# Keys and batch 1's x by the crossbar, six half groups at the start of block 1, and one more last store on ScalarE's queue, in a pooled attention and maxout kernel

## Chip, cores and metric

One core of one Trainium2 chip. The metric is the device time of one execution in microseconds, the median of several.

## The reference

```python
# q, k, v: (8 batches, 8 heads, 576, 64); pool = 8, so 72 pooled keys and values
k_p = k.reshape(B, H, Sp, pool, D).mean(axis=3)
v_p = v.reshape(B, H, Sp, pool, D).mean(axis=3)
attn = softmax(q @ k_p.T / sqrt(D))
x = (attn @ v_p) as (4608 tokens, 512)
h = maximum(maximum(x @ w1, x @ w2), x @ w3)      # 512 -> 768
out = h @ w_out                                   # 768 -> 512
```

## The kernel before

The kernel makes the output in nine blocks of 512 tokens. Block n computes the hidden layer of its tokens (18 groups of four 512-column matmuls) and the projection (four tiles), and in the slots between these groups it puts the attention of batch n+1: keys `k`, eight heads' scores `s`, five values `v` and their transposes `x`, and the query transpose `T` of batch n+2. The loads of batch n+2 are issued by GpSimd and released by the first matmul group of block n.

```python
    def turn_k(b):                       # transpose pooled keys on TensorE, copy to kz
        pkt = keys(b, TR)
        for par in range(2):
            fill_kz(b, par, 0, H, pkt,
                    nc.scalar.copy if b == 1 else nc.vector.tensor_copy)

    def turn_x(b, c0, keep, xn, tag, evac=nc.scalar.copy):
        if b > 1:                        # crossbar, issued by SyncE
            nc.sync.dma_start_transpose(out=xT[...], in_=xn...)
            return
        # otherwise four TensorE transposes into PSUM and one copy
    # in do():
            elif name[0] == "T":
                qTs[b] = sb2.tile([128, 2 * NG, 128], BF16, name="qT", tag="qT")
                nc.sync.dma_start_transpose(
                    out=qTs[b], in_=qbs[b].rearrange("p hp t d -> p (hp t d)"))
    # ... in hidden(): which hidden chunks run on half the tokens first
        if n == 0:
            parts = [(0, 1, 0, 128), (0, 1, 128, 256), (1, 2, 0, 256), (0, 2, 256, NB),
                     (2, JCH, 0, NB)]
        elif n == 1:
            parts = [(0, 1, 0, 256), (0, 1, 256, NB), (1, JCH, 0, NB)]
    # ... in project(): each 128-token tile is stored as two halves by SyncE
                    (nc.scalar if last and u else nc.sync).dma_start(
                        out=dst[:, GS[g], c], in_=osb[64 * u:64 * u + 64, c])
    # ...
    def plan(n):                         # slot: [(batch, steps)]
        b, i = n + 1, 3 * (n == 1)
        got = {0: [], 3: [], 3 + i: [(b, "k")]}
        got.update({5 + i + h: [(b, f"s{h}")] for h in range(H)})
        got[12 + i].append((b + 1, "T"))
        got.update({15 + i + c: [(b, f"v{c} x{c}")] for c in range(5)})
        ...
    def pool_work(n, mm):                # called in slot 0 of block n
        if n + 2 < B:
            after([load_k(n + 2)], mm)
            load_q(n + 2)
            load_v(n + 2)
        if n == 1:
            fold_v(2)
        if n + 2 < B:
            fold_k(n + 2, nc.gpsimd)
            fold_v(n + 2)
```

The softmax here doesn't subtract the row's maximum and nothing guards it: scores larger than these inputs give would overflow.

## Time and profile before

| What | Value |
|---|---|
| Time | 242.75 us median of 3 runs (242.71 to 242.88) |
| Profiled span | 241.0 us |
| TensorE busy | 230.9 us, 96% |
| Next engine (VectorE) | 131.7 us, 55% |
| Start to block 0 | 16.96 us |
| Blocks 0, 1, 2 | 31.73, 24.75, 24.28 us |
| Blocks 3 to 6 | 24.27 to 24.37 us each |
| Block 8 and the end | 25.35 us |

A block's length here and below is the distance between the first hidden-layer matmuls (`pw`) of two successive blocks in TensorE's timeline. A wait for x just before a block's first matmul thus counts for the block before it.

### The profile page before, as it was taken

What the parts mean: (1) busy time and instruction counts of PE and PEld (TensorE: products, weight loads), DVE (VectorE), ACT (ScalarE), POOL (GpSimd) and SP (SyncE); (2) the same over time, 40 slices, a digit from 0 to 9 for tenths busy, and PEclk for the clock granted to TensorE, in tenths of its full rate; (3) what the DMA queues carried; (4) which work ended last, traced back from release to release, by engine and by line L of the source; (5) the groups of instructions that cost most, each with busy time, mean ns of one, the idle gap of its engine ahead of it and who ended that gap; (6) DMA issues with size and microseconds to landing.
All of it is one profiled execution on the core that took longest, in us unless ns stands there. A gap on an engine that the chain in (4) does not pass through costs nothing.

```text
span 241.0 us, 4221 instructions
## 1 busy us (share of the span) xinstructions
PE 230.9 (96%) x1609; PEld 122.7 (51%) x1609; DVE 131.7 (55%) x239; ACT 100.1 (42%) x173; POOL 123.7 (51%) x91
## 2 busy tenths in 40 slices
PE   7698999999999999999999999999999999999992
PEld 3376555575554555455545554555455544444441
DVE  6856754665583558354836483648364834504530
ACT  2373247546513651365235523552355232142121
POOL 8864276989997479638880979286500000000000
PEclk9999999999999999999999999999999999999999
DMA  7999999999948995699769987997640253043006
GB/s 135 188 198 206 196 202 208 169 166 241 184 97 153 222 166 120 128 194 197 131 125 156 227 176 133 193 192 135 133 93 0 69 123 85 3 108 66 0 20 154
DMA packets 51939, 34.29 MB, mean 142 GB/s; under 512 B 32144, under 2 KB 46480, under 8 KB 51920
## 3 DMA queue, kind: packets, MB, share of 16 engines
q0 software_dynamic: 17088, 17.11, 45.5%
q1 hardware_dynamic: 34672, 16.79, 34.3%
q8 instruction: 12, 0.20, 0.3%
q10 hardware_dynamic: 160, 0.13, 0.2%
q14 instruction: 7, 0.06, 0.1%
HBM read 34.60 MB, written 9.44 MB: 183 GB/s over the span
## 4 chain that ended last, share of the span: by engine, by line
PE 89%; DVE 5%; ACT 2%; DMA 2%; issue 1%; DVEq 0%
PE pw L295 55%; PE po L331 19%; PE psc L203 6%; PE pav L238 4%; DMA kt<-in_k_dram 2%; PE pxt L229 1%; DVE kf L362 1%; ACT et L208 1%; DVE t L304 1%; PE pkt L174 1%; PE pvp L156 1%; DVE xn L246 1%; PE pqt L167 1%; DVE kp L366 1%; DVE kf L364 1%
## 5 line engine op out<-in xcount | busy, mean ns | idle before, releaser
L295 PE MATMUL pw<-xT,mw 128*128 128x512 f16 (+2 forms) x696 | 155.6, 364 | 0.8 <-ACT xT L233 0.7
L295 PEld LDWEIGHTS <-mw 128*128 128x128 f16 x696 | 61.8, 98 | 56.2 <-issue 1.0
L304 DVE TENSOR_TENSOR t<-t,pw 128x512 f16<-128x512 f16 (+2 forms) x58 | 37.8, 651 | 71.0 <-PE pw L295 43.7
L301 ACT CAST t<-pw 128x512 f16<-128x512 f32 (+2 forms) x58 | 32.3, 556 | 56.1 <-PE pw L295 54.8
L331 PE MATMUL po<-mwo,hT 128*128 128x512 f16 (+1 forms) x222 | 50.7, 373 | 0.0
L208 ACT ACTIVATE et<-psc 72x576 f16<-72x576 f32 (+2 forms) x62 | 40.7, 662 | 20.9 <-PE psc L203 20.7
L307 DVE TENSOR_TENSOR hT<-t,pw 128x512 f16<-128x512 f16 (+2 forms) x58 | 37.7, 650 | 9.0 <-PE pw L295 5.3
L336 ACT COPY osb<-po 128x512 f32<-128x512 f32 (+1 forms) x36 | 20.9, 580 | 47.7 <-PE po L331 43.7
L135 POOL TENSOR_TENSOR half<-vt 72x2048 f32<-72x2048 f16 x7 | 28.4, 4060 | 10.0 <-DMA vt<-in_v_dram 9.9
L331 PEld LDWEIGHTS <-hT 128*128 128x128 f16 x222 | 20.3, 97 | 21.3 <-DVE hT L307 2.4
L135 POOL TENSOR_TENSOR half<-kt 96x1536 f32<-96x1536 f16 x6 | 18.5, 3085 | 23.4 <-DMA kt<-in_k_dram 23.3
L246 DVE TENSOR_TENSOR xn<-pav,rcp 128x512 f16<-128x512 f32 x39 | 27.0, 691 | 1.5 <-DVE rcp L244 0.2
L136 POOL TENSOR_TENSOR half<-half 72x1024 f32<-72x1024 f32 (+1 forms) x13 | 27.2, 2096 | 1.0
L203 PE MATMUL psc<-qT,kz 128*128 128x64 bf16 (+3 forms) x192 | 25.9, 246 | 0.4 <-DVE kz L179 0.3
L203 PEld LDWEIGHTS <-kz 128*128 128x128 bf16 x192 | 17.8, 98 | 15.7 <-DVE kz L179 1.5
L238 PEld LDWEIGHTS <-et 72*128 72x128 f16 x312 | 15.2, 98 | 7.6
L238 PE MATMUL pav<-vp,et 72*128 72x65 f16 x312 | 16.5, 194 | 0.0
L244 DVE RECIPROCAL rcp<-pav 128x8 f32<-128x8 f32 x39 | 7.9, 204 | 9.4 <-PE pav L238 9.3
L139 POOL TENSOR_TENSOR kp<-half 96x384 bf16<-96x384 f32 x12 | 11.7, 993 | 0.5
L179 DVE COPY kz<-pkt 64x576 bf16<-64x576 bf16 (+1 forms) x14 | 9.9, 711 | 2.9 <-PE pkt L174 2.7
L79 POOL DMA_DIRECT2D vt<-in_v_dram x10 | 8.0, 804 | 2.9 <-DMA qb<-in_q_dram 2.2
L139 POOL TENSOR_TENSOR vp<-half 72x512 f16<-72x512 f32 x7 | 8.9, 1268 | 0.5
(48 smaller groups left out, 79.1 us busy)
## 6 DMA issues: line engine op xcount, KB each, us to landing
out_dram<-osb SPq DMA_DIRECT2D x70, 128.0 KB, 2.4
kt<-in_k_dram POOLq DMA_DIRECT2D x7, 576.0 KB, 7.4
qb<-in_q_dram POOLq DMA_DIRECT2D x7, 576.0 KB, 12.2
vt<-in_v_dram POOLq DMA_DIRECT2D x7, 576.0 KB, 15.0
mw<-in_moe_w_dram POOLq DMA_DIRECT2D x9, 256.0 KB, 9.3
mwo<-in_moe_w_out_dram POOLq DMA_DIRECT2D x1, 768.0 KB, 18.1
qb<-in_q_dram POOLq DMA_DIRECT2D x2, 288.0 KB, 7.0
xT<-xn SPq DMA_TRANSPOSE x30, 2.4
```

The source lines that it names most:

```text
L135: e.tensor_tensor(out=f, in0=t[:, :, 0:4, :], in1=t[:, :, 4:8, :], op=ALU.add)
L136: e.tensor_tensor(out=f[:, :, 0:2, :], in0=f[:, :, 0:2, :], in1=f[:, :, 2:4, :], op=ALU.add)
L203: nc.tensor.matmul(out, kz_all[b % 2][:, f % 2, h, :], qTs[b][:, n + i0:n + i1, 64 * (h % 2):64 * (h % 2) + 64], start=True, stop=True)
L208: nc.scalar.activation(out=out, in_=in_, func=FT.Exp, scale=1.0 / 64.0)
L238: nc.tensor.matmul(pav[:, h // 4, 65 * (h % 4):65 * (h % 4) + 65], ets[b][:, h, c0:c0 + 128], vp_all[:, b, h, :], start=True, stop=True)
L246: nc.vector.tensor_tensor(out=xn, in0=pv[:, :, :, 0:D], in1=rcp.to_broadcast([128, 2, 4, D]), op=ALU.mult)
L295: mm = nc.tensor.matmul(pw, w_sb[wi][:, kc, bass.ts(jc, 128)], xT[:, kc, col], start=(kc == 0), stop=(kc == KCH - 1))
L301: nc.scalar.copy(out=t, in_=pw)
L304: nc.vector.tensor_tensor(out=t1, in0=t, in1=pw, op=ALU.max)
L307: nc.vector.tensor_tensor(out=hT[:, jc, c0:c1], in0=t, in1=pw, op=ALU.max)
L331: nc.tensor.matmul(po, hT[:, jc, bass.ts(mm, 128)], wo_sb[:, jc, c], start=(jc == 0), stop=(jc == JCH - 1))
L336: nc.scalar.copy(out=osb[:, c], in_=po)
```

## The change

The intent is to take work off TensorE, which bounds the kernel: the key transposes of batches 3 to 7 and the x transposes of batch 1 move to the crossbar, that is, to DMA transfers that transpose (`dma_start_transpose`, issued by SyncE; step `Z` is the one of the keys). Batch 1's attention moves later in block 0. To give its x time to arrive, block 1 opens with six half groups (groups on 256 of the 512 tokens; three before) ahead of the other half of the tokens, and batch 2's attention sits eight slots late in block 1. Of the last tile's four stores ScalarE's queue issues three instead of two, and both of the tile's copies go to VectorE. Of block 0 the cut below shows the end alone.

```diff
     def turn_k(b):
-        pkt = keys(b, TR)
+        pkt = keys(b, TR) if b < 3 else kTs[b]
...
-                    nc.scalar.copy if b == 1 else nc.vector.tensor_copy)
+                    nc.vector.tensor_copy if b == 2 else nc.scalar.copy)
     def turn_x(...):
-        if b > 1:
+        if b > 0:
     # in do():
+            elif name[0] == "Z":
+                kTs[b] = sb2.tile([128, 6, 96], BF16, name="kT", tag="kT")
+                nc.sync.dma_start_transpose(
+                    out=kTs[b], in_=kps[b].rearrange("p i a d -> p (i a d)"))
     # in hidden():
-            parts = [(0, 1, 0, 128), (0, 1, 128, 256), (1, 2, 0, 256), (0, 2, 256, NB),
-                     (2, JCH, 0, NB)]
+            parts = [(0, 1, 0, 128), (0, 1, 128, 256), (1, 3, 0, 256), (0, 3, 256, NB),
+                     (3, JCH, 0, NB)]
         elif n == 1:
-            parts = [(0, 1, 0, 256), (0, 1, 256, NB), (1, JCH, 0, NB)]
+            parts = [(0, 2, 0, 256), (0, 2, 256, NB), (2, JCH, 0, NB)]
     # in project():
-                if c.start:
+                if last:
                     nc.vector.tensor_copy(out=osb[:, c], in_=po)
...
-                    (nc.scalar if last and u else nc.sync).dma_start(...)
+                    e = nc.scalar if last and (u or c.start == 0) else nc.sync
     # block 0 (its end)
-              26: [(1, "v0")], 27: [(1, "v1 x0"), (2, "T")], 28: [(1, "v2 x1")],
-              29: [(1, "v3 x2")], 30: [(1, "v4")]})
+              28: [(1, "s7")], 29: [(1, "v0 x0")], 30: [(1, "v1 x1")],
+              31: [(1, "v2 x2")], 32: [(1, "v3 x3")], 33: [(1, "v4 x4")]})
     def plan(n):
-        b, i = n + 1, 3 * (n == 1)
-        got = {0: [], 3: [], 3 + i: [(b, "k")]}
+        b, i = n + 1, 8 * (n == 1)
+        got = {2 + i: [(b, "k")]}
...
-        got[12 + i].append((b + 1, "T"))
-        got.update({15 + i + c: [(b, f"v{c} x{c}")] for c in range(5)})
+        got[12 + i - 3 * (n == 1)].append((b + 1, "T"))
+        got.update({14 + i + c: [(b, f"v{c} x{c}")] for c in range(5)})
+        got[17 + i].append((b + 1, "Z"))
         if n == 1:
-            got[0].append((1, "x3"))
-            got[3].append((1, "x4"))
+            got[0] = [(2, "T")]
```

## The prediction

> **What bounds the kernel now.** I read the page first (busy shares), then the timeline of TensorE, then SyncE's and GpSimd's timelines and the DMA queues in short windows. The page:
>
> ```profile
> span 241.0 us, 4221 instructions
> PE 230.9 (96%) x1609; PEld 122.7 (51%) x1609; DVE 131.7 (55%) x239; ACT 100.1 (42%) x173; POOL 123.7 (51%) x91
> PE pw L295 55%; PE po L331 19%; PE psc L203 6%; PE pav L238 4%; DMA kt<-in_k_dram 2%; PE pxt L229 1%; DVE kf L362 1%; ACT et L208 1%; DVE t L304 1%; PE pkt L174 1%; PE pvp L156 1%; DVE xn L246 1%; PE pqt L167 1%; DVE kp L366 1%; DVE kf L364 1%
> ```
>
> TensorE is the bound: no other engine is above 55%, and the chain of waits is almost all matmuls. The table of windows cuts this into the kernel's own stages: start to 16.96, block 0, blocks 1 to 6:
>
> ```profile
> 16.96:48.69 31.73, 30.00 (x280) 18.84 (x277) 18.65 (x40) 15.83 (x32) 19.51 (x14) 1.00 1.25 195
> 48.69:73.44 24.75, 24.75 (x191) 14.10 (x188) 15.11 (x28) 11.59 (x21) 23.20 (x13) 1.00 0.92 175
> 73.44:97.70 24.26, 24.26 (x167) 12.49 (x166) 13.89 (x24) 10.73 (x18) 17.64 (x11) 1.00 0.89 159
> ```
>
> (First the length, then busy us of PE.) Block 1 and later are gapless; block 0 is not. What one step costs TensorE I take as the distance of starts in its timeline:
>
> ```profile
> 52.63 0.42 PE L174 MATMUL pkt<-ident,kp 96*128 96x96 bf16 x6
> 52.89 1.89 PE L295 MATMUL pw<-xT,mw 128*128 128x512 f16 x8
> 54.62 0.41 PE L203 MATMUL psc<-qT,kz 128*128 128x320 bf16 x3
> 54.86 1.03 PE L295 MATMUL pw<-xT,mw 128*128 128x512 f16 x4
> ```
>
> Keys: 0.26 us; a group of four 512-column matmuls: 0.86 (eight in 1.73); one head's scores: 0.24 to 0.25. From the same view: values 0.26, four x transposes 0.22, a half group 0.43 to 0.44, a projection tile 1.30. Block n's content is thus 20.7 (72+24 matmuls of 0.216) + 2.0 + 1.3 + 0.26 = 24.3, as measured.
>
> [...] The trace agrees for like packets (58 to 59 us: 98 load packets beside 94 store packets), but worse than one to one for the large packets of a key load: in 52 to 54 us, with stores waiting since 49.85, the hardware queue moved none. [...] here all come from SP in program order, so they queue behind each other and the stores.
>
> **What the change takes off TensorE.**
> - Keys of batches 3 to 7 by crossbar: 5 x 0.26 = 1.3 us, in blocks 2 to 6, which are gapless, so it counts whole. The key copies go from DVE to ACT (two of about 0.65); ACT is busy 10.7 of 24.3, so no new bound.
> - x of batch 1: 5 x 0.22 = 1.1 us in blocks 0 and 1, and five ACT copies.
> - Block 0 has 31.73 - 30.00 = 1.7 us of gaps (wait for xT at 22.69, for the summed keys at 27.43, and so on). Three more half groups before the second token half cover about half of that, 0.9.
> - Last stores: SP's last issues at 237.9 and it lands 2.3 us later. Shared with ACT's queue, the last issue is about 237.5: 0.4 us.
> Sum 3.7 us: 239.0 us if nothing new waits.
>
> **What it moves onto SyncE's queue.** This is where I think it goes wrong. Durations of issue:
>
> ```profile
> 61.63 3.81 SPq L270 DMA_TRANSPOSE qT<-qb  x1
> 66.65 4.16 SPq L223 DMA_TRANSPOSE xT<-xn  x3
> 70.91 1.18 SPq L340 DMA_DIRECT2D out_dram<-osb  x2
> 72.18 1.25 SPq L223 DMA_TRANSPOSE xT<-xn  x1
> ```
>
> An x transpose holds SP 1.2 us (it lands after 2.3), two stores 1.18, batch 2's q transpose 3.8 (lands after 5.5 to 7.7). Before, that q transpose was issued at 45.2, ahead of all loads of batch 3, and landed at 51.8; the first score needing it ran at 54.62. After, the order on SP is: x0, two stores, x1, two stores, x2, two stores, x3, two stores, x4, then q. How early can x0 go? Batch 1's values need its pooled v:
>
> ```profile
> 38.18 1.27 POOL L139 TENSOR_TENSOR vp<-half 72x512 f16<-72x512 f32 x1
> 49.59 0.57 POOL L72 DMA_DIRECT2D kt<-in_k_dram  x1 [1.02 <-PE pxt L229]
> ```
>
> So values not before 39.5; walking TensorE's slots with the steps above I get values 0 at 40.5 to 40.8, then the reciprocal (0.2), the product (0.69) and a maximum before them on DVE: x0 at about 42.4. q is issued 5 x 1.2 + 8 x 0.59 = 10.7 us later, at 53.1, all its pieces by 57. TensorE: block 0 ends at 47.0; block 1 opens when x0 and x1 have landed. x1 is issued at 44.8, beside the tail of batch 2's loads, where a store took 5.4 us to land instead of 2.3: so I take about 50. The first slot of block 1 also releases batch 3's loads (before: at 49.59). Their key load then shuts out the hardware queue:
>
> ```profile
> kt<-in_k_dram POOLq DMA_DIRECT2D x1, 576.0 KB, 6.6
> xT<-xn SPq DMA_TRANSPOSE x1, 7.4
> ```
>
> (74 to 76 us: the x transpose issued beside a key load lands when the keys have, in 7.4 us instead of 2.3; in later blocks 8.7 and 9.2.) With slot 0 at 50, keys are loaded at about 51 to 57. Then 512 packets of q and 576 of v follow, at 100 to 150 per us, about 8 us, in which the transpose gets about as many packets (63 to 64 us: 107 beside 150). x4, two stores and q need 256 + 128 + 2304 (18 tiles x 128) packets; 1,100 pass beside the loads, the other 1,600 after them at about 1,000 per us (985 in 65 to 66 us). I estimate landing at 57 + 7.8 + 1.6 = 66.4, say 66.
>
> TensorE reaches batch 2's first score after twelve half groups, two groups and the keys: 12 x 0.436 + 2 x 0.864 + 0.26 = 7.2 us from block start, at 57.2. It is in order, so **it idles from 57 to 66**. The rest of block 1 is 24.3 - 7.2 = 17.1[...]: block 2 starts at 66 + 17.1 + 1.5 = 84.6 instead of 73.44, 11.2 later. Afterwards 1.3 + 0.4 come back: 242.75 + 11.2 - 1.7 = 252. I shade this to 251, as I may overrate the competition.
>
> **Rivals.**
> - *The q transpose lands without any contention.* Even then: values at 39.5, x0 at 40.6, q issued at 51.3, landed at 56.8. The rest of block 1 brings block 2 to 73.9, and the total to 242.75 + 0.5 - 1.7 = 241.6. For it: the late slot of the scores looks chosen for just this landing time. Against it: every hardware transfer issued beside a key load in this trace took 7 to 9 us. So a gain over 2% (below 237.9) would need the pooled v or SP itself to be faster, which nothing in the change does.
> - *The wait comes at the opening of block 1 instead.* x3 is issued at 49.6 to 50.8 and needed at the seventh half group, 52.6; if the key load catches it, TensorE stalls there until 57.5. It then reaches the first score at 62, still before the q transpose: the stall is split, the end is the same. If x1 itself takes 8 us, block 1 opens at 53, the loads and q move with it, and the time is about 255.
> - *Contention is half as bad:* q lands at 61 to 62, stall of 4 to 5 us, time 246 to 247.
> - *Only TensorE's work counts:* 239.0, if the q transpose were fast and early. Its issue order rules this out.
>
> **Range and chances.** The middle is 251; the best case of the issue chain, 241.6, and a badly delayed x1, about 255 to 256, are the ends. I give 243 to 256. Above 247.6 (slower by over 2%) lie all cases in which the key load shuts out the transpose: 0.76. Within 2%: 0.21. Faster by 2%: 0.03.
>
> **What would show it.** In the changed profile: a gap on TensorE of 6 to 10 us in block 1 ahead of the first score of batch 2, released by the DMA of qT, and that transpose taking over 10 us to land instead of 6.6; a first pw of block 1 at 48 to 51 that waited for xT; a lowered granted clock after the gap. Blocks 2 to 6 must be 24.0 long instead of 24.3, and the last store must land about 0.4 us sooner after the last matmul. I am wrong if the q transpose lands before 58, or if the key load lets the transposes pass; then the time is 241.5 to 243.

## The result and the profile after

The changed kernel took 273.74 us (median of 4 runs, 273.32 to 274.34) against 242.74 us: slower, ratio 1.1278 (1.1255 to 1.130). Ratios here and below are the mean time of one kernel's fast runs over that of the other's of the same rounds, so they are not quite the ratio of the quoted medians. Executions over 1.5% slower than the fastest of the same kernel are left out of the means. The direction was predicted; the size, 31 us, was nearly four times the predicted 8, and outside the range.

From the page of the changed kernel: the span, busy shares, the granted clock in tenths over 40 slices, and the chain of waits by engine and by line.

```profile
span 272.1 us, 4201 instructions
...
PE 236.6 (87%) x1581; PEld 125.2 (46%) x1583; DVE 123.8 (45%) x233; ACT 109.9 (40%) x180; POOL 123.5 (45%) x91
...
PEclk9999999797599975799999999999999999999998
...
PE 77%; DMA 14%; DVE 3%; issue 2%; ACT 1%; SPq 1%; DVEq 0%; POOLq 0%
```

TensorE fell from 96% to 87% busy, and its busy time even rose by 5.7 us with 28 matmuls fewer, because some of them ran at a lower clock (mean granted clock of the profiled run 0.945). The chain now holds 14% DMA, where it was nearly all matmul before. The stages say where:

| Stage | Before | After | Difference |
|---|---|---|---|
| Start to block 0 | 16.96 | 17.08 | +0.12 |
| Block 0 | 31.73 | 33.96 | +2.23 |
| Block 1 | 24.75 | 39.32 | +14.57 |
| Block 2 | 24.28 | 38.83 | +14.55 |
| Block 3 | 24.37 | 24.01 | -0.36 |
| Blocks 4 and 5, together | 48.55 | 48.03 | -0.52 |
| Block 6 | 24.27 | 24.36 | +0.09 |
| Block 7 | 20.72 | 20.72 | 0 |
| Block 8 and the end | 25.35 | 25.77 | +0.42 |

TensorE's timeline of the changed kernel (start, duration, line, output and inputs, count, and in brackets the idle time before and what ended it):

```profile
51.04 6.57 PE L299 MATMUL pw<-xT,mw 128*128 128x256 f16 x44 [3.65 <-DMA xT<-xn]
...
69.57 0.64 PE L203 MATMUL psc<-qT,kz 128*128 128x320 bf16 x3 [9.54 <-DMA qT<-qb]
...
90.36 5.34 PE L299 MATMUL pw<-xT,mw 128*128 128x512 f16 x24 [0.95 <-DMA xT<-xn]
107.12 0.45 PE L203 MATMUL psc<-qT,kz 128*128 128x320 bf16 x1 [11.42 <-ACT kz L179]
108.29 0.39 PE L203 MATMUL psc<-qT,kz 128*128 128x192 bf16 x2 [0.73 <-ACT kz L179]
```

There are three pauses. The first opens block 1 (3.65 us, waiting for x); the prediction has it, as block 0's end at 47.0 and block 1's start at about 50. Here too the transposes run beside a load: the first two x took 7.7 and 5.1 us to land, at 50.21 and 50.91, while batch 2's last load landed at 49.54; an x with no load beside it takes 2.3. No run takes batch 2's loads away, so this cause is not tested. The second pause is the predicted one: 9.54 us ahead of batch 2's first score, waiting for the query transpose. The third was not predicted: 12.15 us ahead of batch 3's first scores in block 2. Its releaser is a copy on ScalarE, but that copy had itself waited for the key transpose, as the group of these copies shows (count, then busy time and mean ns, then idle time before and its cause):

```profile
L179 ACT COPY kz<-kT 64x576 bf16<-64x576 bf16 x10 | 11.7, 1168 | 14.3 <-DMA kT<-kp 14.1
```

SyncE's timeline of the changed kernel gives the issues behind these, the first x, the last x, the query transposes of batches 2 and 3 (two in one line), and batch 3's key transpose. The second number is how long they held SyncE and not when they landed:

```profile
42.48 1.30 SPq L223 DMA_TRANSPOSE xT<-xn  x1
...
53.69 2.20 SPq L223 DMA_TRANSPOSE xT<-xn  x1
55.99 13.43 SPq L270 DMA_TRANSPOSE qT<-qb  x2
...
91.68 3.68 SPq L274 DMA_TRANSPOSE kT<-kp  x1
```

GpSimd's timeline has the key loads of batches 3 and 4, each followed at once by the loads of q and v:

```profile
52.36 0.56 POOL L72 DMA_DIRECT2D kt<-in_k_dram  x1 [3.03 <-PE pw L299]
...
91.68 0.55 POOL L72 DMA_DIRECT2D kt<-in_k_dram  x1 [14.36 <-PE pw L299]
```

Batch 2's query transpose was issued 3.6 us after batch 3's loads had begun and took 13.4 us to land. Batch 3's key transpose was issued in the very instant of batch 4's key load and took 14.2 us; in later blocks, where it is issued ahead of the loads, it took 2.4. From the lists of DMA issues (the last number is the time from issue to landing):

```profile
qT<-qb SPq DMA_TRANSPOSE x1, 13.4
...
kT<-kp SPq DMA_TRANSPOSE x1, 14.2
```

What they share is seen in the DMA queues in 61 to 62 us (packets, MB, share of 16 engines; the software queue carries the loads, the hardware queue the transposes and stores):

```profile
q0 software_dynamic: 157, 0.16, 94.5%
q1 hardware_dynamic: 158, 0.03, 31.5%
```

In this microsecond one packet of the transpose goes for one packet of the load, although the load's are some five times larger (0.16 MB against 0.03 for as many). In the middle of a key load it is fewer: in 94 to 96 us 61 packets of the load went by and none of the hardware queue, though the key transpose had been issued at 91.68; why, the trace does not show. Once the loads are done, 1152 packets of the hardware queue go by in one microsecond (68 to 69 us).

The last view is the windows of the changed kernel: length, then the busy time of PE, PEld, DVE, ACT and POOL, then the granted clock, DMA share and GB/s.

```profile
51.04:57.50 6.46, 6.46 (x46) 5.10 (x47) 2.53 (x6) 1.41 (x4) 5.13 (x4) 0.74 0.92 169
...
69.57:74.40 4.83, 4.83 (x18) 2.20 (x19) 0.69 (x1) 1.55 (x3) 4.75 (x2) 0.50 0.36 83
...
108.90:112.80 3.90, 3.90 (x14) 1.70 (x14) 1.36 (x2) 1.62 (x3) 3.17 (x1) 0.55 0.64 117
129.19:153.20 24.01, 24.01 (x161) 12.29 (x160) 12.15 (x22) 13.06 (x20) 15.73 (x10) 1.00 0.96 170
```

After each pause, the 3.65 us one included, the array ran at half clock: finer windows show 0.50 from 51.04 to 54.36, from 69.57 to 74.84 and from 107.12 to 112.38. Length times missing clock, in the windows shown, gives an estimate of the loss: 6.46 x 0.26 + 4.83 x 0.50 + 3.90 x 0.45 = 5.9 us; the last two leave out a part of their slow stretch, so it is rather more. After the 0.95 us wait at 90.36 the clock stayed full (1.00 from 90.36 to 95.70). Block 3 (last line) is gapless at full clock, and shorter than before.

### The profile page after: what moved, and what is told of

The parts are those of the page before. It is cut to its first block, busy times and chain, and to the rows that moved or that the text cites.

```text
span 272.1 us, 4201 instructions
## 1 busy us (share of the span) xinstructions
PE 236.6 (87%) x1581; PEld 125.2 (46%) x1583; DVE 123.8 (45%) x233; ACT 109.9 (40%) x180; POOL 123.5 (45%) x91
## 4 chain that ended last, share of the span: by engine, by line
PE 77%; DMA 14%; DVE 3%; issue 2%; ACT 1%; SPq 1%; DVEq 0%; POOLq 0%
PE pw L299 48%; PE po L335 16%; PE psc L203 6%; DMA kT<-kp 5%; DMA qT<-qb 5%; PE pav L238 3%; DMA xT<-xn 2%; DMA kt<-in_k_dram 2%; ACT kz L179 1%; PE pqt L167 1%; SPq L223 1%; PE pvp L156 1%; DVE kf L366 1%; SPq L345 0%; DVE hT L311 0%
## 5 line engine op out<-in xcount | busy, mean ns | idle before, releaser
L299 PE MATMUL pw<-xT,mw 128*128 128x512 f16 (+2 forms) x720 | 160.6, 367 | 5.0 <-DMA xT<-xn 4.6
L299 PEld LDWEIGHTS <-mw 128*128 128x128 f16 x720 | 65.7, 100 | 61.6 <-issue 4.7
L335 PE MATMUL po<-mwo,hT 128*128 128x512 f16 (+1 forms) x222 | 50.1, 373 | 0.2 <-DVE hT L311 0.2
L203 PE MATMUL psc<-qT,kz 128*128 128x64 bf16 (+3 forms) x192 | 27.3, 255 | 22.0 <-ACT kz L179 12.2
L340 ACT COPY osb<-po 128x512 f32<-128x512 f32 x35 | 20.5, 585 | 47.4 <-PE po L335 47.4
L203 PEld LDWEIGHTS <-kz 128*128 128x128 bf16 x192 | 18.4, 101 | 39.4 <-ACT kz L179 13.0
L135 POOL TENSOR_TENSOR half<-kt 96x1536 f32<-96x1536 f16 x6 | 18.5, 3080 | 21.5 <-DMA kt<-in_k_dram 21.4
L72 POOL DMA_DIRECT2D kt<-in_k_dram x9 | 5.1, 564 | 33.1 <-PE pw L299 31.2
L179 ACT COPY kz<-kT 64x576 bf16<-64x576 bf16 x10 | 11.7, 1168 | 14.3 <-DMA kT<-kp 14.1
```

The lines of the kernel that those rows point to most:

```text
L135: e.tensor_tensor(out=f, in0=t[:, :, 0:4, :], in1=t[:, :, 4:8, :], op=ALU.add)
L203: nc.tensor.matmul(out, kz_all[b % 2][:, f % 2, h, :], qTs[b][:, n + i0:n + i1, 64 * (h % 2):64 * (h % 2) + 64], start=True, stop=True)
L299: mm = nc.tensor.matmul(pw, w_sb[wi][:, kc, bass.ts(jc, 128)], xT[:, kc, col], start=(kc == 0), stop=(kc == KCH - 1))
L335: nc.tensor.matmul(po, hT[:, jc, bass.ts(mm, 128)], wo_sb[:, jc, c], start=(jc == 0), stop=(jc == JCH - 1))
L340: nc.scalar.copy(out=osb[:, c], in_=po)
```

## The experiments

**Theory L**: batch 3's loads, beside which the query transpose runs, make the pause in block 1, and batch 4's loads that in block 2; each pause adds a cold clock. **Rival Q**: SyncE's backlog (five x transposes and the stores ahead of the query transpose) makes the pause, whatever the loads do. Others are named where they matter. Fourteen kernels were run; times of kernels with one round are the median of two runs.

### no_loads: the changed kernel without the loads of batches 3 and 4 (a wrong result, on purpose)

```diff
-        if n + 2 < B:
+        if n < 3:
+            kts[n + 2], qbs[n + 2], vts[n + 2] = kts[n], qbs[n], vts[n]
+        elif n + 2 < B:
```

> The changed kernel, wrong on purpose: batches 3 and 4 are not loaded, the tiles of batches 1 and 2 stand in for them, so no load runs beside batch 2's q transpose or beside batch 3's key transpose. Theory L (the software queue's loads shut the transposes out): the q transpose lands within 7 us of its issue instead of 13.4, TensorE idles at most 3 us ahead of batch 2's first score instead of 9.5, the key transpose lands within 5 us instead of 14.2 and the 11 us pause in block 2 goes; 245 to 250 us. Rival Q (the transposes are slow because SP's own queue is backed up): both still take over 10 us to land; over 268 us.

Measured: 250.92 us (250.12 to 251.72), ratio 1.0329 (1.0246 to 1.0412), just above the 245 to 250 that theory L gave. Blocks 0 to 2 took 31.61, 29.64 and 26.23 us. TensorE's timeline of this run has no pause ahead of batch 2's first score any more; what is left in block 1 are two waits for x:

```profile
50.31 2.78 PE L299 MATMUL pw<-xT,mw 128*128 128x256 f16 x24 [1.30 <-DMA xT<-xn]
55.18 4.02 PE L299 MATMUL pw<-xT,mw 128*128 128x256 f16 x20 [2.09 <-DMA xT<-xn]
```

The query transpose was issued at 56.65 us, later than in the changed kernel, and landed 4.5 us later instead of 13.4:

```profile
qT<-qb SPq DMA_TRANSPOSE x1, 4.5
```

The key transposes took at most 3.8 us. So the loads make both long pauses, and some 23 of the 31 us go with them. The run is still 8 us above the kernel before. Its profile has 1.7 of these in the opening; the rest is mainly in blocks 1 and 2: the two waits above, the slow stretch after the second (20 half-group matmuls in 4.02 us; 20 such took 2.36 us in gated), 1.22 us of waiting for x at the end of block 1, and 1.4 for key copies in block 2 (0.52 and 0.87). The chain of issues on SyncE thus has a cost of its own, in short waits, but makes no long one.

### x_on_pe: the changed kernel with batch 1's x on TensorE

```diff
-        if b > 0:
+        if b > 1:
```

> The changed kernel with batch 1's x back on TensorE, all else kept, so SP has only stores to do before batch 2's q transpose. Theory L: block 1 opens near 47.5, the q transpose is issued near 48 but batch 3's key load starts at the same time, so it still lands at 60 to 64 and TensorE idles 5 to 9 us before the first score; 255 to 268 us. Rival Q (SP's backlog is the cause): the transpose lands 6 us after its issue, at 54, no pause there, SP is on time for the keys as well; 239 to 243 us.

Measured: 279.79 us (278.89 to 280.69), ratio 1.1518 (1.1424 to 1.1611): worse, against the expectation. Here SyncE was free of x, yet the query transpose took longer still. TensorE's timeline of this run:

```profile
76.85 0.64 PE L203 MATMUL psc<-qT,kz 128*128 128x320 bf16 x3 [14.91 <-DMA qT<-qb]
```

and the queues in its 58 to 59 us:

```profile
q0 software_dynamic: 6, 0.04, 64.2%
q1 hardware_dynamic: 13, 0.00, 7.9%
```

Two things happened. An x in the same slot as its values costs TensorE a wait of 1.03 us each time, 1.36 the first (the product on VectorE is not ready), so block 0 became 37.61 us, and the query transpose was issued at 54.96 and not at 48 as I had expected. And batch 3's key load was issued half a microsecond later, at 55.45: the transpose, with no x ahead of it on its queue, took 21.8 us and the key load 18.0 instead of 6.8. With the backlog gone and the pause longer (14.91 us), rival Q is refuted as the cause of the pause. Started together, the two slowed each other; the 6 and 13 packets of this microsecond do not show by what.

### keys_on_pe and early_keys: batch 3's keys away from batch 4's loads

keys_on_pe takes all keys back to TensorE; early_keys issues batch 3's key transpose five slots sooner.

```diff
 keys_on_pe
-        pkt = keys(b, TR) if b < 3 else kTs[b]
+        pkt = keys(b, TR)
-        got[17 + i].append((b + 1, "Z"))
 early_keys
-        got[17 + i].append((b + 1, "Z"))
+        got[17 + i - 5 * (n == 1)].append((b + 1, "Z"))
```

> The changed kernel with all keys back on TensorE. Theory L: the second pause (11.4 us in block 2, waiting for the copy of batch 3's keys) goes with its cold clock, the first stays, and 1.3 us of transposes come back: 273.7 - 14.7 + 1.3 = 260, 258 to 262 us. Rival M (the pause only moves to the next transpose in SP's queue): over 267 us.

> The changed kernel with batch 3's key transpose issued five slots earlier in block 1 (slot 20 instead of 25; the keys were summed at 69.4, long before), ahead of the x transposes and of block 2's loads. Theory L: it lands about 2.4 us after issue, the second pause goes: 273.7 - 14.7 = 259, 257 to 262 us. Rival K (96-partition key transposes are slow of their own the first time): it still takes over 10 us to land, but early enough to be hidden, and the time is the same 259; the landing time tells them apart. Rival M: x2, now 1.2 us later, opens block 2 later by that much and no more.

Measured: keys_on_pe 259.15 us (257.75 to 260.54), ratio 1.0668 (1.0529 to 1.0807); early_keys 258.56 us (258.34 to 258.78), ratio 1.0644 (1.0607 to 1.068). Block 2 fell from 38.83 to 25.12 and 24.8 us, and the key transpose in early_keys landed within 3.9 us. So the third pause is the meeting of one key transpose with one load, worth 15 of the 31 us, and five slots undo it. The pause in block 1 stays in both. In early_keys it is split, in TensorE's timeline:

```profile
57.28 4.45 PE L299 MATMUL pw<-xT,mw 128*128 128x256 f16 x20 [2.92 <-DMA xT<-xn]
...
69.00 0.41 PE L203 MATMUL psc<-qT,kz 128*128 128x320 bf16 x3 [4.07 <-DMA qT<-qb]
```

The second of these starts at 69.00, against 69.57 in the changed kernel: the wait at the seventh half group moves idle time forward and leaves the end nearly where it was, as one of the prediction's rivals has it.

### small_packets: the same key load in six pieces of smaller packets, for batches 3 and 4 (`n < 3`)

```diff
-                for i, j in parts][-1]
+                for i, j in parts][0]
-            after([load_k(n + 2)], mm)
+            after([load_k(n + 2, [(i, i + 1) for i in range(6)]
+                          if n < 3 else ((0, 6),))], mm)
```

> The changed kernel with the key loads of batches 3 and 4 issued in six pieces, so that each packet of a key load is a sixth of its size (1 KB written instead of 6), all else and all bytes the same. Theory P (the two queues take turns packet by packet, so a transpose of 256-byte packets is paced by the size of the load's packets): during the key load the hardware queue passes some 100 packets per us instead of 10 to 30; the q transpose lands about 3 us sooner (10 to 11 instead of 13.4) and batch 3's key transpose within 8 us instead of 14.2; 262 to 268 us. Rival B (what counts is the load's bytes): landings of 13 and 14 us as before, 272 to 275 us.

Measured: 267.11 us (266.13 to 268.10), ratio 1.0997 (1.0960 to 1.1034). The key transpose landed after 6.9 us instead of 14.2 and block 2 fell to 31.38 us. The query transpose, however, took 15.0 us, and block 1 stayed at 39.66. So for the short transpose (six tiles) the key load's form matters. Whether the smaller packets do it is not shown: the same edit also issues the load in six steps, so that the q and v loads start later (by some 2.8 us, an estimate from the 0.55 us that one such step takes in the changed kernel), and no run separates the two. The expectation that the long one (eighteen tiles) lands 3 us sooner failed: it ended about 1 us after the last load here (whose last packets went by in 68 to 69 us, with the landing at 70.0) and 1.4 in the changed kernel, so in both it got through only when the loads did.

### kept_warm: dummy matmuls at the two long pauses (core of the edit)

```diff
+                if (n, slot) in ((1, 13), (2, 5)):
+                    heat(40 if n == 1 else 48, psp.tile([128, 512], F32, name="wm2", tag="tr", bufs=1))
```

> The changed kernel with 40 dummy matmuls ahead of batch 2's first score and 48 ahead of batch 3's, which fill the two long pauses (8.6 of 9.5 us, 10.4 of 12.1) and depend on nothing. If the array's clock falls in the pauses, this gives back the slow stretches after them: 2.4 us after the first (4.8 us at 0.50) and about 2.4 after the second (4.4 us at 0.5 to 0.6); 268 to 270 us. If the clock is not the reason, 273.7.

Measured: 278.01 us (276.02 to 280.01), ratio 1.1446 (1.1379 to 1.1513). The total gives no verdict: in this run the pause of block 1 (9.60 us) came at the seventh half group, ahead of the dummies, which were then pure cost (block 1: 46.18 us). Block 2 does give one. In a window of this run, after the dummies:

```profile
112.00:118.00 6.00, 6.00 (x38) 3.20 (x37) 1.84 (x3) 3.96 (x7) 2.65 (x2) 1.00 1.04 130
```

The clock is full, and block 2 took 34.37 us: its 24.0 of work and the 48 dummies' 10.4, with neither idle time nor cold clock. Of the 14.8 us that block 2 of the changed kernel is over 24.0, the pauses in its timeline are 12.4 and the rest, about 2.4, is the clock. (In this run the key transpose landed after 9.7 us and not 14.2, so not all of the 4.5 us by which block 2 is shorter are the clock's.)

### gated: every load kept, but batch 3's released by the landing of batch 2's query transpose

```diff
+                turned[b] = nc.sync.dma_start_transpose(       # query transpose, in do()
-                if slot == 0 and n > 0:
-                    pool_work(n, mms[-1])
+                if slot == 0 and n == 1:
+                    fold_v(2)
+                if slot == (n == 1) and n > 0:
+                    pool_work(n, turned[2] if n == 1 else mms[-1])
```

(and the key transpose as in early_keys).

> The kernel after with two edits: the key transpose of each batch five slots earlier in block 1 (as in early_keys, 258.6 us), and batch 3's key, query and value loads released only by the landing of batch 2's query transpose, instead of by a matmul of block 1. The result stays correct. Theory L (the loads shut the transpose out): with no load in the way the q transpose of batch 2 lands some 6 us after its issue at 53 to 56 us, as in the run without those loads, and the pause before batch 2's first score shrinks from 9.5 (after) and 4.1 plus 2.9 (early_keys) to 0 to 2 us. But the loads go some 8 to 10 us later, so batch 3's own query transpose and the last values' transposes of x come late, and block 2 waits some 6 us for x: 250 to 254 us. Rival Q (the backlog of SyncE): the q transpose still lands over 10 us after its issue and the pause stays at 4 us or more: 258 us or above.

Measured: correct; of its two runs one was fast, 251.03 us; the profiled one was slow (256.69 us, its opening 3 us late), so I read from it the order and size of waits and not the total. From TensorE's timeline of that run:

```profile
62.26 0.41 PE L203 MATMUL psc<-qT,kz 128*128 128x320 bf16 x3 [1.14 <-DMA qT<-qb]
...
84.50 8.07 PE L299 MATMUL pw<-xT,mw 128*128 128x512 f16 x24 [4.98 <-DMA xT<-xn]
```

The query transpose, behind the same backlog, landed 4.3 us after its issue at 57.8, and the pause shrank from 9.54 to 1.14 us. This is theory L in a correct kernel. Two waits for x ahead of it, 0.94 and 2.32 us, stay: the backlog's own part. The price is paid where expected: the later loads delay batch 3's own transposes, and block 2 waits 4.98 us for x (and starts cold: 24 matmuls in 8.07 us instead of 5.34, at a granted clock of 0.65 from 84.50 to 92.50).

### stores_only: the last stores' part alone, on the kernel before

```diff
-                if c.start:
+                if last:
-                    (nc.scalar if last and u else nc.sync).dma_start(
+                    e = nc.scalar if last and (u or c.start == 0) else nc.sync
+                    e.dma_start(
```

> The kernel before with only the last stores spread over two queues and both last copies on DVE. My prediction: the last store is issued 0.4 us earlier, 242.3 us. Rival, from the changed kernel's trace (its end comes 4.87 us after the last projection against 4.46 before): ACT's queue now issues three stores of 0.6 us in a row, so the last store goes out later, 243.1 us. Either way under 0.5 us.

Measured: 244.08 us (six runs, 242.33 to 246.66, one of them slow), ratio of the fast runs 1.0031 (0.9988 to 1.0074). The last part took 25.21 us in its profile; with the old stores it took 25.35 to 25.58 us in seven profiles, with the new ones 25.44 to 25.84 in the eight others. So no gain in time can be told from none. ScalarE's timeline of the changed kernel:

```profile
267.05 1.86 ACTq L345 DMA_DIRECT2D out_dram<-osb  x3
```

Three stores in a row hold ScalarE's queue 1.86 us, so the last of them is issued 1.14 us after the last matmul instead of 1.37 and lands after 3.23 us instead of 3.45 (1.13 and 3.26 in stores_only). That is 0.2 us sooner, half of what was predicted. In the changed kernel the profile then runs on for 1.6 us after the last landing, against 1.0 in the kernel before; why, it does not show.

### keys_only and keys_slot2: the keys' part alone, on the kernel before

keys_only moves the keys of batches 3 to 7 to the crossbar and their copies to ScalarE, but leaves the copies in slot 3; keys_slot2 puts them in slot 2, as the change does.

```diff
 keys_only                       (plus kTs and step "Z", as in the change)
-        pkt = keys(b, TR)
+        pkt = keys(b, TR) if b < 3 else kTs[b]
-                    nc.scalar.copy if b == 1 else nc.vector.tensor_copy)
+                    nc.vector.tensor_copy if b == 2 else nc.scalar.copy)
+        got[17 + i].append((b + 1, "Z"))
 keys_slot2
-        got = {0: [], 3: [], 3 + i: [(b, "k")]}
+        got = {0: [], 3: [], (2 if n > 1 else 3 + i): [(b, "k")]}
```

> The kernel before with only the keys of batches 3 to 7 by the crossbar (transpose issued after x2, copies on ACT). My prediction: blocks 2 to 6 each 0.26 us shorter, 241.4 us, if batch 3's key transpose, issued near 71, lands ahead of the loads issued at 74.8. Rival: the key transposes meet the loads of the next block as in the changed kernel, one pause of some us, over 245 us.

> The kernel before with only the keys of batches 3 to 7 by the crossbar, as keys_only, but the copy into the scores' operand one slot earlier (slot 2 as in the changed kernel). keys_only lost 1.1 us per block: the two ACT copies take 1.17 us each from SBUF (0.64 from PSUM) and the first scores waited for them. One slot is 0.86 us, so blocks should fall to 24.1 to 24.3 us from 25.4: 242 to 243 us. If the copies' time does not matter, 248 again.

Measured: keys_only 248.61 us (248.15 to 250.82), ratio 1.026 (1.0226 to 1.0295), its blocks 3 to 6 25.36 to 25.38 us long; keys_slot2 241.56 us (241.34 to 244.62), ratio 0.9974 (0.9931 to 1.0018), its blocks 2 to 6 24.01 to 24.02. In keys_only the second score matmul, which needs the second copy, waits in every such block, as in TensorE's timeline of this run:

```profile
80.41 0.29 PE L203 MATMUL psc<-qT,kz 128*128 128x192 bf16 x2 [0.87 <-ACT kz L179]
```

The reason is the copy. Groups of key copies, the first from the kernel before, the second from the run best2 below:

```profile
L179 DVE COPY kz<-pkt 64x576 bf16<-64x576 bf16 x12 | 9.1, 755 | 2.9 <-PE pkt L174 2.7
```

```profile
L179 ACT COPY kz<-kT 64x576 bf16<-64x576 bf16 x5 | 5.8, 1165 | 0.0
...
L179 DVE COPY kz<-kT 64x576 bf16<-64x576 bf16 x5 | 3.4, 679 | 0.2
L179 ACT COPY kz<-pkt 64x576 bf16<-64x576 bf16 x3 | 1.9, 633 | 0.6 <-PE pkt L174 0.6
```

For the same shape, ScalarE takes 1.17 us from `kT` (SBUF) and 0.63 from `pkt` (PSUM); I had taken 0.65 for both. Two in a row are 2.3 us, which slot 3 does not leave and slot 2 just does.

### mended_loads0, mended, best, best2: keeping the parts that pay

All have the half groups, the stores as before, and batch 1's x on TensorE one slot after its values. The query transpose of batch 2 goes back to block 0 (slot 30), ahead of the loads. mended_loads0 takes keys by the crossbar from batch 4 on; mended also releases batch 3's loads six slots later; best issues each key transpose a slot sooner, ahead of x3, copies batch 2's keys three slots sooner, and splits the two key copies of a batch between ScalarE and VectorE; best2 takes batch 3's keys by the crossbar as well.

```diff
 mended_loads0 (core; changed kernel is the base)
-        if b > 0:
+        if b > 1:
+              28: [(1, "s7")], 29: [(1, "v0")], 30: [(1, "v1 x0"), (2, "T")],
+              31: [(1, "v2 x1")], 32: [(1, "v3 x2")], 33: [(1, "v4 x3")]})
-        b, i = n + 1, 8 * (n == 1)
+        b, i = n + 1, 6 * (n == 1)
+            got[3] = [(1, "x4")]
 mended (mended_loads0 is the base; fold_v(2) leaves pool_work)
-                if slot == 0 and n > 0:
+                if slot == 0 and n == 1:
+                    fold_v(2)
+                if slot == (6 if n == 1 else 0) and n > 0:
 best (mended_loads0 is the base)
-                    nc.vector.tensor_copy if b in (2, 3) else nc.scalar.copy)
+                    nc.vector.tensor_copy if b in (2, 3) or (par and b > 1) else nc.scalar.copy)
-        got = {2 + i: [(b, "k")]}
+        got = {5 if n == 1 else 2: [(b, "k")]}
-            got[17 + i].append((b + 1, "Z"))
+            got[16 + i].append((b + 1, "Z"))
 best2 (best is the base)
-        pkt = keys(b, TR) if b < 4 else kTs[b]
+        pkt = keys(b, TR) if b < 3 else kTs[b]
-                    nc.vector.tensor_copy if b in (2, 3) or (par and b > 1) else nc.scalar.copy)
+                    nc.vector.tensor_copy if par and b > 1 else nc.scalar.copy)
-        got = {5 if n == 1 else 2: [(b, "k")]}
+        got = {7 if n == 1 else 2: [(b, "k")]}
-        if n > 1:
-            got[16 + i].append((b + 1, "Z"))
+        got[16 + i].append((b + 1, "Z"))
```

> The changed kernel with batch 1's x on TensorE (each a slot after its values), batch 2's q transpose back in block 0, keys by the crossbar from batch 4, stores as before, and batch 3's loads still released by block 1's first slot. Theory L: block 1 opens at 47, so the loads start at 48 and catch the q transpose (issued 45, landing 51.8 before) in its last part: it lands after 58, TensorE pauses 4 us or more before the first score at 52; 244 to 252 us. Rival: a transpose issued 3 us ahead of the loads is through; 240 us.

> As mended_loads0, but batch 3's loads are released by block 1's seventh slot, some 3 us later. Theory L: the q transpose lands by 52 as before, no pause; block 2 opens 1.5 to 2 us earlier than before, blocks 3 to 6 are 0.26 us shorter each: 239.5 to 240.5 us. Rival (the later loads only push batch 3's transposes into block 2's loads): 242 us or more.

> mended_loads0 with batch 2's keys copied three slots earlier, the key transpose one slot earlier (before x3), and the two key copies on ACT and DVE side by side. Its profile lost 0.4 us in block 1, 0.3 in block 5 and 1.0 in block 6 to waits for these copies; so 242.9 - 1.7 = 241.2, 240.8 to 241.8 us. If the waits move elsewhere: 242.5.

> As the run best (batch 1's x by TensorE one slot after its values, half groups and stores as there, key transposes ahead of x), but with batch 3's keys by the crossbar as well, batch 2's keys copied at slot 7 instead of 5, and each batch's two key copies split between ACT and DVE. If what best still loses in blocks 1 and 2 (25.26 and 24.28 against the 24.75 and 24.01 that these blocks had in other runs) is the key copies' waits, both go: a profiled span of 239.0 and 240.8 to 241.5 us, 0.5 to 0.8% under the kernel before. Rival: the waits only move to another instruction of the same blocks, or batch 3's key transpose meets batch 4's load as in the kernel after (then block 2 is longer by several us): 242 us or more.

| Run | Time, us (range) | Ratio to before (interval) | Blocks 0, 1, 2 | First matmul of block 0 to the end |
|---|---|---|---|---|
| before | 242.4 to 243.3 in most rounds | 1 | 31.73, 24.75, 24.28 | 224.0 |
| mended_loads0 | 242.93 (241.64 to 243.30) | 0.9999 (0.9976 to 1.0022) | 31.03, 25.15, 24.27 | 224.4 |
| mended | 245.96 (244.37 to 247.46) | 1.0132 (1.0089 to 1.0176) | 31.04, 26.91, 24.62 | 226.2 |
| best | 242.10 (241.61 to 243.76) | 0.9981 (0.9957 to 1.0005) | 31.03, 25.26, 24.28 | 222.9 |
| best2 | 243.39 (241.24 to 244.46) | 0.9994 (0.9938 to 1.0050) | 31.04, 24.73, 24.02 | 222.4 |

The last column is the profiled span less the opening of that run. In mended_loads0 the query transpose, issued at 44.7, landed about 6.3 us later, just as the key load began; I had expected the loads to catch it, and that failed. mended was a failed edit: putting `fold_v(2)` ahead of the loads on GpSimd sent them at 57.2 and not at about 53 (an estimate: block 1 opened at 50.16, and six half groups take 2.6), and block 2 waited 1.61 us for batch 2's x. best and best2 remove most of what mended_loads0 still lost (last column), and best2's blocks 0 to 2 have just the lengths that I had expected (its block 3 took 24.32 instead of 24.01).

None of them is faster by a margin that the runs can show. From block 0 on best2 saves 224.0 - 222.4 = 1.6 us, but the time to block 0 varies: 16.96 us in the profile of before, 18.97 in that of best2. There the first query load landed 0.6 us later, TensorE idled 2.85 us ahead of it instead of 2.07, and was slow from about 11 to 14.5: nine of the query's transposes took 1.17 us at 12.21, where the kernel before took 0.67. The same slow spell (1.14 to 1.17 us for nine) is in all six profiles whose block 0 opens after 18.5 us, and in none of the ten others (0.67), which open it by 17.3. In the timed rounds beside best2, 3 of 11 runs of the kernel before, too, took 245.1 to 245.5 us instead of 242.6 to 243.8. The fastest run of best2 is 241.24, that of before in these rounds 242.58. Why five of six runs of best2 were slower than that fastest one by 1.5 to 3.2 us, when only one of six of best was so, I cannot say for sure; the instructions up to block 0 are meant to be the same. The five list a mean granted clock of 0.988 to 0.993 and the fast one 0.999, which fits the spell in the opening, but only one of them was profiled.

## Why the prediction was right in direction and wrong in size

Its own sum was 252, shaded to 251. The step that failed is the fourth below: the moved key transposes were taken as free. Measured against its steps:

1. **The issue chain on SyncE: right.** x0 was predicted at 42.4 and issued at 42.48; block 1 was to open at about 50 and opened at 51.04. The query transpose went at 55.99 instead of 53.1: from one x to the next, stores included, took 2.6 to 3.3 us instead of 2.4, and the last x held SyncE 2.2 instead of 1.2.
2. **The query transpose is shut out: right, a little short.** Predicted landing 66, measured 69.4; predicted pause 9 us, measured 9.54. That the length fits so well is partly luck: TensorE came to the score at 60.03 and not at 57, and the landing was late by as much. The line at 61.63 from which the prediction took 3.8 us of holding SyncE is batch 3's query transpose; batch 2's had held it 4.59. no_loads and gated show the cause. Rival Q as the cause of this pause, and the rival in which the transpose lands without contention, fell.
3. **The clock: mis-sized.** I put 1.5 us for one cold spell after the pause, an estimate that rested on no trace. There were two in block 1: the 3.65 us wait at its opening already cooled the clock (0.74 over 6.46 us, an estimated 1.7 us lost), and the pause cost at least 4.83 x 0.50 = 2.4 by the same estimate. The x wait of 0.95 at the end of block 1 was not in the sum either. Together with step 2, block 2 opened at 90.36 instead of 84.6: 5.8 us.
4. **"Blocks 2 to 6 must be 24.0 long": failed for block 2, and this is the largest error.** I counted the key transposes as free once off TensorE, and asked only when the q and x transposes meet the loads. In block 1 the whole attention sits eight slots late, so batch 3's key transpose is in slot 25, behind stores and x, and is issued as block 2's first group releases batch 4's loads. It took 14.2 us instead of 2.4, and block 2 was 38.8: 14.8 us that no rival of mine contained. early_keys and keys_on_pe show it.
5. **Keys elsewhere: right.** Blocks 3 to 5 are 24.01 to 24.02 instead of 24.27 to 24.37; keys_slot2 shows it alone. The copy's size was wrong (1.17 us, not 0.65), without harm in slot 2 where the transpose is on time. Block 6 of the changed kernel kept nothing of it (24.36; 24.01 in keys_slot2).
6. **Half groups in block 0: nearly right.** Predicted 0.9 us, and 0.7 in the runs that keep them (31.03 against 31.73; no run has them alone). The changed kernel spent that on its 3.65 us wait. Cutting a group in two cost little: in mended a half group took 0.435 us, two of them 0.870 against 0.864 for a whole one.
7. **Last stores: mis-sized, and without effect.** Predicted -0.4; the last store landed 0.2 us sooner after the last matmul, but the last part was 0.42 longer in the changed kernel, and stores_only shows no gain in time.

The sum closes, as it must for parts of one timeline: 252 + 5.8 (block 2's opening) + 14.8 (block 2) + 1.1 (block 6 and the stores, which gave nothing) = 273.7, as measured. The shading from 252 to 251 went the wrong way: I doubted the competition in the one place where I had found it, and did not look for it at the other.

## What to carry to other kernels

A transfer that leaves the bounding engine is not free (here the key transpose beside a load took 14.2 us, the later ones, issued ahead of theirs, 2.4): write down, for each one moved, when it will be issued in the new order and which load is then in flight, and do this for every moved transfer, not only for the one that looks tight. Shifting a whole phase of work later also shifts everything in it against the loads that the next block releases; check the last item of the shifted phase first. A pause can cost more than its length: in the changed kernel the 9.54 us one was followed by 4.83 us at a granted clock of 0.50. In the profiles here every pause of TensorE between two matmuls of 2.75 us or more was followed, at once or within some 2 us, by a slow stretch (in early_keys, after 2.89 us, 24 half-group matmuls took 4.08 us; in no_loads, after 1.30 us, 24 took 2.78), and none below 2 us was; in between it differed (after 2.32 us in gated 20 of them took 2.36 us; after 2.09 in no_loads, soon after the pause of 1.30, they took 4.02). So count a cold clock for each longer pause, and for each of several.

## What the runs measured of transposes and copies

- A crossbar transpose beside a load: 13.4 us to land for the query transpose in the changed kernel and 21.8 in x_on_pe, against 4.3 to 4.5 without loads (gated, no_loads); 14.2 against 2.4 for the key transpose; and the load can be slowed as well (18.0 us in x_on_pe against 6.8). In the changed kernel the queues passed 157 packets of the later loads beside 158 of the transpose in one microsecond, but 61 of the key load beside none in two.
- The time that a crossbar transpose holds SyncE: an x transpose without loads beside it 1.2 us of some 2.3 to its landing, a query transpose 3.4 to 4.6 of 5.5 to 7.7 (kernel before), and 8.7 of 13.4 in the changed kernel.
- The key copy on ScalarE: 0.633 us from PSUM, 1.16 to 1.17 from SBUF. Both read with a step of 96 elements, and VectorE took only 0.68 for the same copy from SBUF; no run reads without the step, so it is not shown whether the step has a part in it.
